# When v is loaded, how a product is cut, and where a split stands: LSH attention and expert layers on one core

## The chip, the cores and the metric

One NeuronCore of a Trainium2 chip runs the whole program. The metric is the device time of one execution in microseconds; before the change it is 791.69 us, the median of 3 runs (791.14 to 792.95).

## The reference

For 2 batches of 8 heads (768 rows, 64 columns) the attention is masked by hashes: q and k are multiplied by a 64 x 6 matrix, the signs are six bits, and a score counts only where the bits of q and of k agree. The result goes through 4 experts (512 to 1024 to 512) whose outputs are added with normalized weights.

```python
mask = q_bucket[:, :, :, None] == k_bucket[:, :, None, :]
scores = np.where(mask, scale * q @ k.T, -1e9)
attn = softmax(scores)
x = (attn @ v), heads side by side           # (1536, 512)
for e in range(4):
    out += p[:, e:e+1] * (np.maximum(x @ w1[e], 0) @ w2[e])
```

## The kernel before

**Attention** (`attention`, from line 470 on) runs over all 16 heads of both batches in steps: six tiles t of 128 rows each make one head, so a step is a (batch, head, t). In each step a list of letters, `ORDER = "VUXSRMENP"`, issues one piece each of several stages, some of them lagging behind by a fixed number of steps:

- S, `stage_s`: TensorE multiplies q by k into a large PSUM tile `sps` (lines 357 and 359, two matmuls of 384 columns each); VectorE takes the minimum with the mask's bound into `p` (line 364).
- E, `stage_e`, one step later: ScalarE's exponential (line 380).
- X, `stage_x`, two steps later in batch 0: VectorE turns blocks of 32 x 32 of `p` into `pt` (line 411).
- N, `stage_n`, three steps behind the end of a head: VectorE's reciprocal of the sums, and SyncE stores it in a row in DRAM (line 392). R, `stage_r`, one step later: SyncE loads that row back, broadcast over 64 partitions, as `rdb` (line 399).
- V, `stage_v`, from three steps behind the end of the odd head of a pair: TensorE multiplies the turned probabilities of both heads by v (line 428), 192 small matmuls (the trace has two records for each) that go to four row groups and two column groups of the array. In batch 0 the product of the first three pairs is cut into `V_PARTS` = 4 parts, one a step; the last pair of batch 0 and batch 1 have it in one.
- U, `stage_u`: ScalarE brings the product from PSUM to `xf` (line 449). M, `stage_m`: POOL multiplies it by `rdb` and splits it in a high and a low part, in two halves (lines 458, 460, 463).
- P: one piece of `prep_head`, which prepares the next head while this one is under way. Transposes of q and k into PSUM (`tps`, line 298), a split in high (ScalarE, line 229) and low (VectorE, line 230) parts, copies on POOL (line 220), the hash matmuls (`hps`, line 314), ScalarE's sign (line 322), POOL's bits (line 328) and a copy. The two large PSUM tiles in flight (pool `ps2`) serve `sps`, `tps` and `hps` in turn. In P also stand two loads on SyncE: q and k of the head after the next at t = 1 (`load_qk`, line 200), and v of the next head at t = 4:

```python
if t == 4 and x + 1 < len(hseq):
    load_v(*hseq[x + 1])
```

`load_v` (line 208) issues four DMAs of 192 KB, one for each group of 32 partitions, into a tile `tv` of which there are two. SyncE takes its instructions in order: one that waits holds up all behind it.

**Expert layers** (`moe`, `second_layer`, and `moe_fast` for batch 1) multiply in high and low parts, three matmuls for one. Weights come through `load_w` (line 553, SyncE) into two buffers `ws` and are split by `split_w`.

**The driver** at the end runs attention of batch 0 alone, with the first weights' split among its steps; then the expert layers of batch 0, into which the steps of batch 1's attention are put by cost: a step counts 652, a product `2 * PV_COST`, and after each group of matmuls so many steps follow as keep the ratio `ATT_PACE * n_att / n_moe`, where `n_att` contains `PV_COST` too. Then come batch 1's expert layers alone.

Of the kernel before, what the change touches and what calls it, by code (L numbers as in the profile page):

```python
# [22 lines left out]
LAG_R = 4  # L23
LAG_X = (2, 3)
LAG_V = (3, 4)
V_PARTS = 4
PV_COST = 3840
PP_BUFS = 4
QK_AT = 1
BLOCKS_FROM = 11  # L30
# [14 lines left out]
def tile_lsh_attention__then__domain_moe(  # L45
# [12 lines left out]
    B, H, S, D = q.shape  # L58
# [37 lines left out]
    def big(name):  # L96
        return ps2.tile([P, 2, 512], F32, tag="big", name=name)

    def one(name):
        return ps1.tile([P, 512], F32, tag="one", name=name)  # L100
# [15 lines left out]
    def two(t):  # L116
        return t.rearrange("p (a n) -> p a n", a=2)
# [65 lines left out]
    def in_blocks(b, h):  # L183
        return b * H + h >= BLOCKS_FROM
# [20 lines left out]
    def load_v(b, h):  # L205
        t = ld.tile([P, QD, NT, D], F32, tag="tv", name="tv", bufs=2)
        for a in range(QD):
            nc.sync.dma_start(
                out=t[a * 32 : (a + 1) * 32], in_=v[b, h].rearrange("(r k c) d -> k r c d", r=QD, c=NT)
            )  # L210
        vvs[b, h] = t
# [3 lines left out]
    def stack_tiles(b, h):  # L215
        heads[b, h] = tuple(stk.tile([P, S], F32R, tag=n, name=n) for n in ("q1", "al", "ah", "k2"))
        return heads[b, h]

    def copy_pool(dst, src):
        nc.gpsimd.tensor_scalar(out=dst, in0=src, scalar1=1.0, scalar2=1.0, op0=ALU.mult, op1=ALU.mult)  # L220
# [7 lines left out]
    def split_half(dst_hi, dst_lo, src):  # L228
        nc.scalar.activation(dst_hi, src, ACTF.Copy, scale=qk_scale)  # L229
        nc.vector.scalar_tensor_tensor(  # L230
            out=dst_lo, in0=src, scalar=qk_scale, in1=dst_hi.bitcast(F32), op0=ALU.mult, op1=ALU.subtract
        )
# [49 lines left out]
    def prep_head(b, h):  # L282
        second = (b, h) == (0, 1)
        if not second:
            tqk = loaded.pop((0, b, h))
        q1, al, ah, k2 = stack_tiles(b, h)
        if second:
            for ps, sl in zip(in_psum, halves):
                split_half(ah[:, sl], al[:, sl], ps[:, :NH])
        elif in_blocks(b, h):  # L290
            xt = ld.tile([P, S], F32, tag="tqk", name="xt")
            nc.vector.transpose(out=xt, in_=tqk.rearrange("p c r d -> p (c r d)"))
            yield 0
            split_half(two(ah), two(al), two(xt))
        else:
            ps = big("tps")
            for c in range(NT):
                nc.tensor.transpose(
                    ps[:, c // 3, (c % 3) * P : (c % 3 + 1) * P], tqk[:, c].rearrange("p a d -> p (a d)"), ident
                )  # L300
            split_half(two(ah), two(al), ps[:, :, :NH])
        for rows in (slice(0, D), slice(D, P)):
            copy_pool(q1[rows], ah[0:D].bitcast(F32))
        copy_pool(k2[0:D], ah[D:P].bitcast(F32))
        yield 654
        if second:
            yield 0
            ps = [one("hps1") for _ in range(2)]
        else:
            hps = big("hps")  # L310
            ps = [hps[:, i] for i in range(2)]
        for j, (w, a) in enumerate(((phi, ah), (plo, ah), (phi, al))):
            for i, sl in enumerate(halves):
                nc.tensor.matmul(ps[i][:MKE, :NH], w, a[:, sl], start=j == 0, stop=j == 2)  # L314
        copy_pool(ah[0:D], al[D:P].bitcast(F32))
        if second:
            for i, sl in enumerate(halves):
                nc.scalar.activation(
                    k2[D:MKE, sl], ps[i][D:MKE, :NH], ACTF.Sign, bias=sgn_bias[D:MKE], scale=SGN_SCALE
                )  # L320
        else:
            nc.scalar.activation(
                two(k2[D:MKE]), hps[D:MKE, :, :NH], ACTF.Sign, bias=sgn_bias[D:MKE], scale=SGN_SCALE
            )
        yield 978
        if b and h and not in_blocks(b, h):
            yield 0
        nc.gpsimd.tensor_scalar(
            out=al[D:MKE],
            in0=k2[D:MKE].bitcast(F32),  # L330
            scalar1=1.0,
            scalar2=bit_mul[D:MKE],
            op0=ALU.add,
            op1=ALU.mult,
        )
        copy_pool(k2[MQ:MQE], al[MK:MKE].bitcast(F32))
        yield 0
# [3 lines left out]
    for j in range(KD):  # L341
        t = xp.tile([P, 2, S], F32R, tag=f"x{j}", name="xs0")
# [70 lines left out]
    def parts_of(b, h):  # L413
        return 1 if b or h >= PB else V_PARTS

# [21 lines left out]
    def stage_u(b, j):  # L437
        banks = pvs.pop((b, j))
        for i in range(2):
            vvs.pop((b, 2 * j + i))  # L440
            pts.pop((b, 2 * j + i))
        if b:
            x = xraw[:, j]
        else:
            xf[j] = xs.tile([P, S], F32, tag="xf", name="xf", bufs=1)
            x = xf[j]
        xv = x.rearrange("p (t a q) -> p a t q", t=NT, q=32)
        for a in range(QD):
            nc.scalar.activation(xv[:, a], banks[a][:, : NT * 32].rearrange("p (t q) -> p t q", q=32), ACTF.Copy)
# [19 lines left out]
    hseq = [(b, h) for b in range(B) for h in range(H)]  # L469
# [3 lines left out]
    def attention():  # L473
        n = len(seq)
        prep = [iter(())]

        def do(op, i):
            if op == "N":
                j = i - LAG_N
                if 0 <= j < n and j % NT == NT - 1:  # L480
                    stage_n(*seq[j][:2])
            elif op == "R":
                j = i - LAG_R
                if 0 <= j < n and j % NT == NT - 1:
                    stage_r(*seq[j][:2])
            elif op == "X":
                for b, lag in enumerate(LAG_X):
                    j = i - lag
                    if 0 <= j < n and seq[j][0] == b:
                        stage_x(*seq[j])  # L490
            elif op == "S":
                if i < n:
                    b, h, t = seq[i]
                    if t == 0:
                        x = hseq.index((b, h))
                        prep[0] = prep_head(*hseq[x + 1]) if x + 1 < len(hseq) else iter(())
                    stage_s(b, h, t)
                    return 652
                return DRAIN
            elif op in "VUM":  # L500
                for back in range(min(LAG_V), max(LAG_V) + V_PARTS + 3):
                    j = i - back
                    if not 0 <= j < n or j % NT != NT - 1 or seq[j][1] % 2 == 0:
                        continue
                    b, h, _ = seq[j]
                    part, parts = back - LAG_V[b], parts_of(b, h)
                    if op == "V" and 0 <= part < parts:
                        stage_v(b, h // 2, part, parts)
                        return 2 * PV_COST * b
                    if op == "U" and part == (0 if b else parts):  # L510
                        stage_u(b, h // 2)
                    for g in range(G if op == "M" else 0):
                        if part == (parts if (b, h) == (0, H - 1) else (1 if b else 1 + parts) + g):
                            stage_m(b, h, g)
            elif op == "E":
                j = i - LAG_E
                if 0 <= j < n:
                    stage_e(*seq[j])
            elif op == "P":
                if i < n:  # L520
                    b, h, t = seq[i]
                    c = next(prep[0], None) if t >= PREP_AT else None
                    x = hseq.index((b, h))
                    if t == QK_AT and x + 2 < len(hseq):
                        load_qk(*hseq[x + 2])
                    if t == 4 and x + 1 < len(hseq):
                        load_v(*hseq[x + 1])
                    return c
            return None

        for i in range(n + max(LAG_V) + 4):
            for op in ORDER:
                c = do(op, i)
                if c is not None:
                    yield c
# [345 lines left out]
    with tc.manual_schedule():  # L881
# [6 lines left out]
        i = 0  # L888
# [13 lines left out]
        for _ in sp:  # L902
            pass
        n_att = H * (NT * 652 + 1632 + PV_COST) + (max(LAG_V) + 4) * DRAIN
        n_moe = NU * (NS * FC * 1960 + NS * TS * 2600)
        for b in range(B):
            dm = da = 0.0
            for c in (moe_fast if b else moe)(b, b * NU):
                dm += c
                while da < dm * ATT_PACE * n_att / n_moe:  # L910
                    x = next(att, None)
# [34 lines left out]
```

## Time and profile before

| | |
|---|---|
| median of 3 runs | 791.69 us (791.14 to 792.95) |
| the profiled execution | 791.18 us, its span 789.4 us |
| TensorE (PE), busy | 725.6 us, 92% |
| VectorE (DVE) | 478.0 us, 61% |
| ScalarE (ACT) | 276.1 us, 35% |
| GpSimd (POOL) | 303.6 us, 38% |
| mean granted clock of TensorE | 0.931 |

The span is the time from the first to the last instruction of the profiled execution; 1.8 us of its own time lie around it. Stages are found by when their lines run: batch 0's attention alone ends near 187 us (first expert matmul with all its inputs), batch 1's attention is over by 500. A matmul's duration in the timeline contains its fill, so the distance between starts is read for what one occupies. "x96" counts the trace's records merged in one line, and the bracket at the end of a line is the idle time ahead of it and what ended it.

### The profile page before, as it was taken

The page shows a single profiled execution, that of the slowest core. Times are in us where ns is not written, and L with a number is a line of the kernel's source. Part 1 is how long each engine was busy: PE and PEld are TensorE (multiplying, and loading weights), DVE is VectorE, ACT ScalarE, POOL GpSimd, SP SyncE. Part 2 cuts the span into 40 slices and gives each one's busy share as a digit, 9 for nine tenths or more (in the row PEclk, how much of TensorE's full clock was granted, in tenths as well). Part 3 has the DMA queues.
Part 4 walks back from the last instruction along what each step waited for, and adds up shares of the span by engine and source line. Part 5 has one row for each costly group of instructions (what it writes and reads, how often), then busy time and mean ns, then how long its engine had stood idle before and what let it go on. Part 6 is the DMA issues. An engine that isn't in the chain of part 4 may idle for free.

```text
span 789.4 us, 14887 instructions
## 1 busy us (share of the span) xinstructions
PE 725.6 (92%) x6232; PEld 645.3 (82%) x6232; DVE 478.0 (61%) x766; ACT 276.1 (35%) x542; POOL 303.6 (38%) x279
## 2 busy tenths in 40 slices
PE   7777858685999999999989999999999999999998
PEld 5556646575989898898979989989899899898896
DVE  7846556523662784378158523387776866866853
ACT  5545444421521342053213202044353343433430
POOL 5326263513331551345134114384342433423520
PEclk9685859586999999999999999999999999999999
DMA  9035151625005420740324212224212212312212
GB/s 209 16 63 106 43 126 38 158 49 84 11 2 115 131 57 2 177 111 13 74 77 103 65 55 64 56 77 136 80 54 81 81 53 57 104 45 64 72 36 81
DMA packets 65554, 59.75 MB, mean 76 GB/s; under 512 B 38224, under 2 KB 46672, under 8 KB 65488
## 3 DMA queue, kind: packets, MB, share of 16 engines
q1 hardware_dynamic: 64464, 58.48, 29.1%
q8 instruction: 49, 0.80, 0.4%
q10 hardware_dynamic: 1024, 0.33, 0.2%
q14 instruction: 17, 0.14, 0.1%
HBM read 55.60 MB, written 3.19 MB: 74 GB/s over the span
## 4 chain that ended last, share of the span: by engine, by line
PE 81%; DVE 5%; POOL 4%; issue 4%; DMA 3%; ACT 2%; SPq 1%; DVEq 0%; POOLq 0%; ACTq 0%
PE mps L603 11%; PE mps L604 11%; PE mps L605 11%; PE pv L428 8%; PE mps L664 5%; PE mps L663 5%; PE mps L665 5%; PE sps L359 3%; PE sps L357 3%; PE hps L314 3%; PE mps L818 2%; PE mps L814 2%; PE mps L817 2%; DMA tqk<-in_k_dram 2%; DVE al L230 1%
## 5 line engine op out<-in xcount | busy, mean ns | idle before, releaser
L603 PE MATMUL mps<-w2hi,hb 128*128 128x512 f32 (+1 forms) x388 | 150.9, 389 | 0.0
L604 PE MATMUL mps<-w2lo,hb 128*128 128x512 f32 (+1 forms) x388 | 150.5, 388 | 0.0
L605 PE MATMUL mps<-w2hi,hb 128*128 128x512 f32 (+1 forms) x388 | 150.5, 388 | 0.0
L380 ACT ACTIVATE p<-p,nb 128x768 f32<-128x768 f32 x96 | 89.6, 933 | 74.4 <-DVE p L364 74.1
L364 DVE TENSOR_SCALAR_CACHE_REDUCE p<-sps 128x768 f32<-128x768 f32 x96 | 89.0, 927 | 38.8 <-PE sps L359 38.8
L597 DVE SCALAR_TENSOR_TENSOR acc<-mps,pe,acc 128x512 f32<-128x512 f32 (+1 forms) x85 | 62.9, 741 | 67.1 <-PE mps L605 66.9
L669 ACT ACTIVATE hb<-mps 128x384 fp32r<-128x384 f32 x64 | 31.4, 491 | 204.8 <-PE mps L665 204.8
L663 PE MATMUL mps<-xs,w1hi 128*128 128x384 f32 x256 | 87.7, 343 | 13.4 <-POOL xs L460 10.6
L411 DVE STREAM_TRANSPOSE pt<-p 128x768 f32<-128x768 f32 x96 | 92.7, 965 | 0.4 <-ACT p L380 0.4
L664 PE MATMUL mps<-xs,w1hi 128*128 128x384 f32 x256 | 87.3, 341 | 0.4 <-POOL xs L463 0.4
L665 PE MATMUL mps<-xs,w1lo 128*128 128x384 f32 x256 | 87.1, 340 | 0.0
L605 PEld LDWEIGHTS mps<-w2hi,hb 128*128 128x128 f32 x388 | 72.8, 188 | 15.9
L603 PEld LDWEIGHTS mps<-w2hi,hb 128*128 128x128 f32 x388 | 72.8, 188 | 14.4 <-issue 0.8
L604 PEld LDWEIGHTS mps<-w2lo,hb 128*128 128x128 f32 x388 | 72.9, 188 | 14.0
L800 POOL TENSOR_TENSOR w2lo<-ws,w2hi 128x512 fp32r<-128x512 f32 x32 | 40.5, 1283 | 105.8 <-ACT w2hi L799 105.8
L564 POOL TENSOR_TENSOR w1lo<-ws,w1hi 128x512 fp32r<-128x512 f32 x32 | 41.8, 1308 | 91.2 <-DVE w1hi L572 74.3
L428 PE MATMUL pv<-pt,tv 32*64 32x192 f32 x3072 | 73.4, 336 | 3.2 <-issue 3.0
L428 PEld LDWEIGHTS pv<-pt,tv 32*64 32x64 f32 x3072 | 64.1, 136 | 11.8 <-issue 10.6
L564 POOL TENSOR_TENSOR w2lo<-ws,w2hi 128x512 fp32r<-128x512 f32 x32 | 41.1, 1287 | 82.8 <-DVE w2hi L572 41.3
L357 PE MATMUL sps<-ah,q 128*128 128x384 f32 x192 | 61.8, 408 | 9.1 <-DVE p L364 7.5
L670 DVE SCALAR_TENSOR_TENSOR hb<-mps,hb 128x384 fp32r<-128x384 f32 x64 | 35.2, 554 | 56.8 <-ACT hb L669 56.6
L220 POOL TENSOR_SCALAR q<-ah 64x768 fp32r<-64x768 f32 (+1 forms) x33 | 27.8, 843 | 104.8 <-ACT ah L229 103.5
(127 smaller groups left out, 1287.5 us busy)
## 6 DMA issues: line engine op xcount, KB each, us to landing
ws<-in_moe_w_dram SPq DMA_DIRECT2D x64, 512.0 KB, 3.7
tv<-in_v_dram SPq DMA_DIRECT2D x64, 192.0 KB, 4.6
rdb<-row SPq DMA_DIRECT2D x16, 192.0 KB, 3.5
out_dram<-acc SPq DMA_DIRECT2D x11, 256.0 KB, 2.1
tqk<-in_q_dram SPq DMA_DIRECT2D x10, 192.0 KB, 5.7
tqk<-in_k_dram SPq DMA_DIRECT2D x10, 192.0 KB, 5.7
tqk<-in_q_dram SPq DMA_DIRECT2D x12, 96.0 KB, 4.2
tqk<-in_k_dram SPq DMA_DIRECT2D x10, 96.0 KB, 4.8
```

The lines of the kernel that those rows point to most:

```text
L357: nc.tensor.matmul(ps[:, i, :NH], q1[:, sl], k1[:, i * NH : (i + 1) * NH], start=True, stop=False)
L364: nc.vector.tensor_scalar(out=two(pt), in0=ps[:, :, :NH], scalar1=MASKED, scalar2=MASKED, op0=ALU.min, op1=ALU.min, accum_out=nb,)
L380: nc.scalar.activation(pt, pt, ACTF.Exp, bias=nb, scale=-1.0, accum_out=den[:, t : t + 1])
L411: nc.vector.transpose(out=pts[b, h][:, :, t], in_=p.rearrange("p (k n) -> p k n", n=32))
L428: nc.tensor.matmul(pvs[b, j][a][i * D : (i + 1) * D, : NT * 32], vvs[b, 2 * j + i][rows, r, c], pts[b, 2 * j + i][rows, k].rearrange("p t ...
L564: nc.gpsimd.tensor_tensor(out=lo[:, c - 1], in0=st[c - 1], in1=hi[:, c - 1].bitcast(F32), op=ALU.subtract)
L603: nc.tensor.matmul(ps, hh[:, ts], w2hi[:, f, cs], start=n == 0, stop=False)
L604: nc.tensor.matmul(ps, hh[:, ts], w2lo[:, f, cs], start=False, stop=False)
L605: nc.tensor.matmul(ps, hl[:, ts], w2hi[:, f, cs], start=False, stop=n == FC - 1)
L663: nc.tensor.matmul(ps[:, :SB], w1hi[:, kk, fs], xhi[b, kk][:, sl], start=kk == 0, stop=False)
L664: nc.tensor.matmul(ps[:, :SB], w1hi[:, kk, fs], xlo[b, kk][:, sl], start=False, stop=False)
L665: nc.tensor.matmul(ps[:, :SB], w1lo[:, kk, fs], xhi[b, kk][:, sl], start=False, stop=kk == KD - 1)
```

## The change

Three edits and a cost. `load_v` of the next pair's two heads is called in `stage_u`, right behind the ScalarE copies that take the product from PSUM; of the calls in P only that for head 1 of batch 0 is left. The product of batch 0's first three pairs is cut in two parts. In `prep_head` for batch 0 the generator gives way once more between the transposes and the split, and once between the hash matmuls and the sign, so that each of the latter is issued one step later. `PV_COST` is 1950 where it was 3840; it is used in batch 1's pacing alone.

```diff
-V_PARTS = 4
-PV_COST = 3840
+V_PARTS = 2
+PV_COST = 1950
@@ prep_head
                 nc.tensor.transpose(
                     ps[:, c // 3, (c % 3) * P : (c % 3 + 1) * P], tqk[:, c].rearrange("p a d -> p (a d)"), ident
                 )
+            if not b:
+                yield 0
             split_half(two(ah), two(al), ps[:, :, :NH])
...
         else:
+            if not b:
+                yield 0
             nc.scalar.activation(
                 two(k2[D:MKE]), hps[D:MKE, :, :NH], ACTF.Sign, bias=sgn_bias[D:MKE], scale=SGN_SCALE
             )
@@ stage_u
         for i in range(2):
             vvs.pop((b, 2 * j + i))
             pts.pop((b, 2 * j + i))
+            nxt = b * H + 2 * j + 2 + i
+            if nxt < len(hseq):
+                load_v(*hseq[nxt])
@@ attention, P
-                    if t == 4 and x + 1 < len(hseq):
-                        load_v(*hseq[x + 1])
+                    if (b, h, t) == (0, 0, 4):
+                        load_v(0, 1)
```

SyncE's queue around the second pair's product (heads 2 and 3), before. The first `tv` is v of head 4, `tqk` q and k of head 6, the second `tv` v of head 5; `row` and `rdb` are the reciprocals of head 3.

```order
L208 DMA tv_842<-in_v_dram 32x4x384 x4
L200 DMA tqk_904<-in_q_dram 128x6x64
L200 DMA tqk_904<-in_k_dram 128x6x64
L392 DMA row_972<-rd_970 128x6
L553 DMA ws_976<-in_moe_w2_dram 128x2x512
L399 DMA rdb_826<-row_972 64x768
L208 DMA tv_1098<-in_v_dram 32x4x384 x4
```

The same stretch now, from the broadcast of head 2 (`row_804`) to q and k of head 7 (`tqk_1214`):

```order
L403 DMA rdb_826<-row_804 64x768
L560 DMA ws_883<-in_moe_w2_dram 128x2x512
L200 DMA tqk_892<-in_q_dram 128x6x64
L200 DMA tqk_892<-in_k_dram 128x6x64
L396 DMA row_1008<-rd_1006 128x6
L403 DMA rdb_826<-row_1008 64x768
L208 DMA tv_1129<-in_v_dram 32x4x384 x4
L208 DMA tv_1134<-in_v_dram 32x4x384 x4
L200 DMA tqk_1214<-in_q_dram 128x6x64
L200 DMA tqk_1214<-in_k_dram 128x6x64
```

Both v loads (heads 4 and 5) stand together behind the broadcast of head 3, and q and k of head 6 (`tqk_892`) no longer stand behind a v load but behind a load of weights; those of head 7 now stand behind both v loads.

TensorE in the even head of the second pair, before, from the transposes for the next head on:

```order
L298 MATMUL tps<-ident,tqk 128x128 x6
L357 MATMUL sps<-ah,q_753 128x384 x2
L359 MATMUL sps<-k_756,al 128x384 x2
L314 MATMUL hps<-ah,phi 108x384 x2
L314 MATMUL hps<-ah,plo 108x384 x2
L314 MATMUL hps<-al,phi 108x384 x2
L428 MATMUL pv<-pt,tv 64x192 x48
L357 MATMUL sps<-ah,q_753 128x384 x2
L359 MATMUL sps<-k_756,al 128x384 x2
L428 MATMUL pv<-pt,tv 64x192 x48
L357 MATMUL sps<-ah,q_753 128x384 x2
L359 MATMUL sps<-k_756,al 128x384 x2
```

And now:

```order
L298 MATMUL tps<-ident,tqk 128x128 x6
L361 MATMUL sps<-ah,q_759 128x384 x2
L363 MATMUL sps<-k_762,al 128x384 x2
L432 MATMUL pv<-pt,tv 64x192 x96
L361 MATMUL sps<-ah,q_759 128x384 x2
L363 MATMUL sps<-k_762,al 128x384 x2
L316 MATMUL hps<-ah,phi 108x384 x2
L316 MATMUL hps<-ah,plo 108x384 x2
L316 MATMUL hps<-al,phi 108x384 x2
L432 MATMUL pv<-pt,tv 64x192 x96
L361 MATMUL sps<-ah,q_759 128x384 x2
L363 MATMUL sps<-k_762,al 128x384 x2
```

The hash matmuls stand one score further back, and 96 instead of 48 small matmuls stand between two scores.

SyncE at the last pair of batch 0, before (the reciprocals and the broadcast of head 7 ahead of the v load of head 9):

```order
L392 DMA row<-rd 128x6
L399 DMA rdb<-row 64x768
L208 DMA tv<-in_v_dram 32x4x384 x4
L191 DMA tqk<-in_q_dram 32x24x32 x2
```

And now, where the v loads of heads 8 and 9 have come between the two:

```order
L396 DMA row<-rd 128x6
L208 DMA tv<-in_v_dram 32x4x384 x8
L403 DMA rdb<-row 64x768
L191 DMA tqk<-in_q_dram 32x24x32 x2
```

## Rows read from the trace of the kernel before

**Rows 1.** Windows by stage: us, then busy us (count) of each engine, clock, DMA share, GB/s

```profile
20.00:187.00 167.00, 119.96 (x1822) 96.32 (x1822) 90.81 (x156) 70.89 (x140) 67.48 (x76) 0.70 0.36 79
...
187.00:500.00 313.00, 305.05 (x2902) 279.04 (x2902) 176.43 (x302) 87.65 (x182) 113.91 (x101) 0.99 0.28 70
```

**Rows 2.** SyncE's queue: waits from 20 to 200 us: total, times, longest

```profile
SPq L208 <- PE pv L428: 82.4, 4, 22.3
```

**Rows 3.** Waits of TensorE from 20 to 200 us: total, times, longest

```profile
PE tps L298 <- DMA tqk<-in_k_dram: 18.7, 3, 6.3
...
PE sps L359 <- POOL k L220: 5.9, 3, 2.7
```

**Rows 4.** Timeline near the second pair's end: start us, duration, engine, line, tiles, idle before

```profile
94.08 1.75 SPq L208 DMA_DIRECT2D tv<-in_v_dram  x4
...
95.73 0.08 DVE L364 DVE_READ_ACCUMULATOR p<-sps 128x1 f32 x1
...
96.47 0.65 SPq L200 DMA_DIRECT2D tqk<-in_k_dram  x1
...
101.75 1.51 PE L298 MATMUL tps<-ident,tqk 128*128 128x128 f32 x6 [6.24 <-DMA tqk<-in_k_dram]
```

**Rows 5.** Timeline: transposes of five heads, starts (preparing heads 2, 3, 7, 8, 9)

```profile
19.87 1.54 PE L298 MATMUL tps<-ident,tqk 128*128 128x128 f32 x6 [0.23 <-DVE p L364]
...
32.97 1.54 PE L298 MATMUL tps<-ident,tqk 128*128 128x128 f32 x6 [0.68 <-DVE p L364]
...
117.80 1.48 PE L298 MATMUL tps<-ident,tqk 128*128 128x128 f32 x6
...
141.90 1.51 PE L298 MATMUL tps<-ident,tqk 128*128 128x128 f32 x6 [6.29 <-DMA tqk<-in_k_dram]
...
156.67 1.48 PE L298 MATMUL tps<-ident,tqk 128*128 128x128 f32 x6
```

**Rows 6.** Timeline, VectorE: two minima a step apart; the low part of a split

```profile
112.55 0.92 DVE L364 TENSOR_SCALAR_CACHE_REDUCE p<-sps 128x768 f32<-128x768 f32 x1
...
114.30 0.92 DVE L364 TENSOR_SCALAR_CACHE_REDUCE p<-sps 128x768 f32<-128x768 f32 x1
...
120.38 1.02 DVE L230 SCALAR_TENSOR_TENSOR al<-tps,qk_scale,ah 128x768 fp32r<-128x768 f32 x1 [1.38 <-ACT ah L229]
```

**Rows 7.** Timeline: the first part of a product; one step of a later product

```profile
39.29 3.67 PE L428 MATMUL pv<-pt,tv 32*64 32x192 f32 x96
...
127.84 0.62 PE L357 MATMUL sps<-ah,q 128*128 128x384 f32 x2
...
128.75 2.21 PE L428 MATMUL pv<-pt,tv 32*64 32x192 f32 x96
...
130.88 0.62 PE L357 MATMUL sps<-ah,q 128*128 128x384 f32 x2
...
131.89 0.96 DVE L364 TENSOR_SCALAR_CACHE_REDUCE p<-sps 128x768 f32<-128x768 f32 x1 [1.18 <-PE sps L359]
```

**Rows 8.** Windows: a head with a product and a late transpose; one without

```profile
117.80:143.06 25.26, 18.22 (x427) 15.10 (x426) 12.96 (x22) 9.15 (x19) 8.00 (x9) 0.84 0.32 70
...
143.06:156.67 13.61, 11.31 (x33) 8.67 (x31) 10.81 (x18) 8.00 (x15) 10.45 (x12) 0.50 0.65 155
```

**Rows 9.** Timeline behind the last product of batch 0

```profile
172.57 1.75 SPq L208 DMA_DIRECT2D tv<-in_v_dram  x4
...
175.65 1.50 SPq L392 DMA_DIRECT2D row<-rd  x1
...
181.15 0.48 SPq L399 DMA_DIRECT2D rdb<-row  x1
...
184.52 1.18 POOL L458 TENSOR_TENSOR xf<-xf,rdb 128x384 f32<-128x384 f32 x1 [21.61 <-DMA rdb<-row]
```

**Rows 10.** Timeline in the expert layers of batch 0

```profile
396.20 0.43 DVE L572 CAST w2hi<-ws 128x512 fp32r<-128x512 f32 x1 [18.18 <-DMA ws<-in_moe_w_dram]
...
397.21 0.61 PE L663 MATMUL mps<-xs,w1hi 128*128 128x384 f32 x1 [2.76 <-DVE hb L670]
```

## The prediction

> **What bounds the kernel now.** I read the windows by stage first, then the waits, then the timeline at the places that the waits name. The windows [rows 1] split the span. From 187 to 500 us, the expert layers of batch 0 with the attention of batch 1 among them, TensorE (PE) is busy for 305.05 of 313 us at a granted clock of 0.99: little but less PE work helps there, and what follows, the expert layers of batch 1 alone, the change doesn't touch. From 20 to 187 us, the attention of batch 0, it is busy for 119.96 of 167 us at a granted clock of 0.70, and no other engine is full (VectorE, DVE, 90.81 us). That stretch is where the change can pay.
>
> Who holds it up stands in the waits. SyncE's queue spent 82.4 us in 4 waits of the v load (L208) for the product of the pair [rows 2], and PE waited 18.7 us, in 3 waits of some 6.2, for a landing k half of tqk, and 5.9 us, in 3, for GpSimd (POOL) at the score matmuls [rows 3]. The timeline of one pair joins the two [rows 4]: the v load of the next pair, which sits on SyncE's queue behind nothing but a buffer that this pair's product reads, gets through at 94.08; only then can the q and k of a later head be issued, k at 96.47; it lands 5.2 us later, and the transposes that need it start at 101.75. The PSUM buffer that these transposes take was read out at 95.73 + 0.08 = 95.81, so 5.94 us of the gap is the queue's.
>
> Transposes to transposes, heads 2 to 7 took 156.67 - 32.97 = 123.7 us, 41.2 a pair, and a head with neither product nor late transposes 32.97 - 19.87 = 13.1 us [rows 5]. VectorE's own pace is a step of 114.30 - 112.55 = 1.75 us and 1.02 us a head for the low part of the split [rows 6]: 12 x 1.75 + 2 x 1.02 + 0.4 for two reciprocals = 23.4 us a pair, well below 41.2. So no engine sets the pace; the chain of waits does.
>
> **The change part by part.**
>
> *The v load behind the evacuation.* The order shows it: ahead of the q and k that an even head's step 1 issues no v load stands any more, at most a load of weights, whose buffer POOL frees some four steps before. The 8 v loads now stand behind the pair's last product on TensorE, which is next in the program anyway, so SyncE is held there only as long as TensorE itself is. The q and k of [rows 4] would go out some 5 steps before they are needed. Three waits of 5.94 us go: **-17.8 us**. Late next is VectorE with its 1.75 a step, which is what the next terms are made against. Behind the v loads stand, in an odd head, q and k, the reciprocals' row and its broadcast; none is due before step 5 of that head.
>
> *POOL's waits.* In before, the multiplications of a finished pair (two groups of three operations) come in steps 1 and 2 of the odd head, wait for the broadcast of the reciprocals, which SyncE held back too, and push the sign's two operations behind the next head's scores. With the product done in two steps they come in step 5 of the even head and step 0 of the odd one, after one head's sign operations and before the next's. The 5.9 us of [rows 3] go: **-5.9 us**.
>
> *Split and sign a step later* (six prepared heads, 2 to 7). VectorE stood 1.38 us for ScalarE's high part, which itself had waited for the transposes of the same step [rows 6]. A step later those are long done, but the split then holds one of the two large PSUM buffers until VectorE has read it, so TensorE can run one step less ahead. Between 0 and 1.4 us a head; I take 0.8, since the high part still stands behind an exponential on ScalarE: **-4.8 us**. The two POOL operations behind the sign end a step later, about 1 us before the next head's scores want them; I cost that at nothing, and its cover is the one spare step.
>
> *Product in two parts.* The instructions are the same; what moves is how well VectorE is fed. In before, a product step is TensorE's: scores from 127.84 to 128.75, a part from 128.75 to 130.88, then the next scores, 3.04 us, and VectorE stands 1.18 us in it [rows 7]. Four are 12.2 us. Now two steps have 0.91 + 2 x 2.13 = 5.17 us, and the two that are freed run at VectorE's 1.75: 2 x 5.17 + 2 x 1.75 = 13.8. **+1.7 us a pair, +5.0 us** for three. Below, nothing (TensorE runs ahead in the slack); above, a part that begins at the low clock: 96 records took 3.67 us there against 2.21 [rows 7], 1.46 more on the second half of the first part, 4.4 us for three pairs.
>
> *Start of the expert layers.* The last pair's reciprocals travel to memory and back: v loads at 172.57, row at 175.65, broadcast at 181.15, POOL released at 184.52, 11.95 us behind the end of the product [rows 9]. In the new order the row goes out first, but 8 v loads (twice the 1.75 us of issuing, and 1,536 KB) stand between it and the broadcast. [rows 4] give the rate: 6 transfers of 192 KB, 1,152 KB, from 94.08 to 101.75, 150 KB a us. 1,536 KB take 10.2 us, and with 2 ahead (VectorE's minimum, the reciprocals, the row's issue) and 1.3 for the broadcast's own 192 KB it lands some 13.7 us behind the product, 1.8 later than now; if the transfers share the engines rather than queue, issue at 6.1 + 3.4 gives 9.5, 2.5 earlier. I take **+1 us**, nearer to the queue that [rows 4] show.
>
> *Batch 1.* The same SyncE wait made VectorE, and with it TensorE, late by 2.76 us at 397.21 [rows 10]: VectorE had stood 18.18 us for weights whose load was queued behind v. That goes: **-2.8 us** (bounds 0 and -3.5). The smaller PV_COST spreads attention steps and expert matmuls in another ratio; the work is the same and TensorE is full there, so I cost it at nothing. What covers it is TensorE's own queue of ready work; if it fails, waits like this one come in its place.
>
> **Sum.** -17.8 - 5.9 - 4.8 + 5.0 + 1 - 2.8 = -25.3 us. The profiled execution took 791.18 us (span 789.4, 1.8 around it), 0.5 below the median 791.69 of the runs, within their spread. 791.18 - 25.3 = 765.9: **766 us**. A pair would then take (123.7 - 17.8 - 5.9 - 4.0 + 5.0) / 3 = 33.7 us, or 13.1 and 20.6 for its two heads.
>
> **The rivals.**
>
> *The low clock stays: slower.* [...] **4%**.
>
> *The q and k are late again, behind v.* 8 v loads and a q and k are 1,920 KB, 12.8 us at the rate of rows 4, 16.2 with a load of weights (512 KB) among them. From the end of the product to the next even head's transposes there are about nine steps of 1.75 and a split, 17 us. For it: no row shows ten such transfers in a row, and in the new order q and k of the odd head stand behind all 8. Against: 1 to 4 us of slack. Some 3 us a pair: **775 us**, 13%.
>
> *The two parts eat more.* Both halves of the first part at the low clock, nothing from the later split, half of POOL's waits back: 4.4 + 4.8 + 3: **778 us**, 10%.
>
> *It doesn't take the wait away.* The q and k are late for another reason: only the 2.8 and a little more are gained, **788 us**, 2%. The order speaks against it.
>
> **How the numbers follow.** The forecast has 71%. Its low end: product parts at no cost (-5.0), 1.4 instead of 0.8 a head (-3.6), broadcast early (-3.5), 754 if all come together; the high end is the third rival with batch 1 gaining nothing, 781. The range 756 to 779 takes in the forecast's likely part and most of the second and third rival. A measurement here can tell 0.2%, 1.6 us, from no change. Faster 0.93, same 0.02, slower 0.05.
>
> **What would show it.** Right: no wait of transposes for tqk in 20 to 187 us; SyncE's waits of the v load short, and before q and k none; expert layers' first matmul some 23 us earlier; POOL no releaser of scores; product steps near 5.2 us on TensorE with VectorE idle 2 to 4 us in each. Wrong: the stage still ends at 187 us, or the granted clock in it falls below 0.70, or new waits in 187 to 500 us exceed 5 us.

## The result and the profile after

The changed kernel took **772.78 us** (median of 4 runs, 768.57 to 774.39) against 792.01 us of the kernel before (4 runs beside it, 791.14 to 792.95): a ratio of 0.9749, 95% interval 0.9708 to 0.9789. It is faster by 2.5%, where 766.0 us (756 to 779) had been forecast. The profiled execution took 772.6 us, its span 770.9 us, 18.5 us less than the 789.4 us before.

The page of the changed kernel, busy time of each engine and the granted clock in 40 slices of the span:

```profile
PE 720.2 (93%) x6232; PEld 643.3 (83%) x6232; DVE 473.2 (61%) x766; ACT 276.8 (36%) x542; POOL 303.9 (39%) x279
...
PEclk9587887759999999999999999999999999999999
```

The windows, cut where [rows 5] and [rows 8] cut them before, at the transposes that a head starts with: head 1, heads 2 to 7, and then the stretch from 187 us on, as in [rows 1].

```profile
20.42:34.28 13.86, 11.31 (x37) 9.22 (x37) 11.73 (x21) 8.27 (x15) 5.04 (x6) 0.61 0.33 63
34.28:137.03 102.75, 86.57 (x1369) 70.32 (x1369) 71.16 (x124) 56.32 (x110) 56.68 (x63) 0.78 0.50 102
...
187.00:500.00 313.00, 303.27 (x2913) 277.31 (x2912) 167.96 (x296) 83.80 (x175) 113.56 (x98) 1.00 0.28 73
```

The same view of the kernel before, heads 2 to 7:

```profile
32.97:156.67 123.70, 91.58 (x1369) 73.35 (x1369) 72.65 (x124) 57.02 (x113) 56.81 (x63) 0.69 0.39 86
```

Heads 2 to 7 take 102.75 us where they took 123.7, at a clock of 0.78 instead of 0.69. So a pair takes 34.25 us, not 41.2. That is more than the whole gain. The account of the 18.5 us of span, stretch by stretch:

| stretch | before us | after us | difference |
|---|---|---|---|
| up to head 2's transposes | 32.97 | 34.28 | +1.3 |
| heads 2 to 7 | 123.70 | 102.75 | -20.95 |
| from head 8's transposes to the second matmul of the expert layers (L664 at 187.44, now L671 at 168.42) | 30.77 | 31.39 | +0.6 |
| the rest | 601.96 | 602.48 | +0.5 |

TensorE's waits from 15 to 200 us, which answer to [rows 3] (total, times, longest):

```profile
PE sps L361 <- DVE p L368: 16.2, 26, 1.1
PE mps L670 <- POOL xs L467: 12.3, 1, 12.3
PE tps L298 <- DVE p L368: 4.3, 6, 0.7
```

No transposes wait for a landing any more, and no score matmuls for POOL. What is left is VectorE's minimum, that is, the pace of the pipeline, and the start of the expert layers. SyncE's queue, from 20 to 200 us, in place of the 82.4 us of [rows 2]:

```profile
SPq L396 <- DVE rd L394: 118.2, 9, 30.7
...
SPq L208 <- PE pv L432: 5.2, 3, 2.2
```

The queue still waits, now 118.2 us for the reciprocals (22.0 us before), but no transfer that TensorE needs is late by it: none of TensorE's waits names a DMA. The last reading is of TensorE's waits from 200 to 520 us, the expert layers of batch 0 with the attention of batch 1 in them. Here is something that was not forecast. A wait for "issue" is a pause for which the profile shows nothing that the engine waited for; the first row is of the kernel before, the others are of the changed kernel:

```profile
PE pv L428 <- issue: 3.0, 4, 1.1
```

```profile
PE pv L432 <- issue: 8.1, 7, 1.7
...
PE mps L670 <- issue: 0.6, 1, 0.6
```

The wait for late weights of [rows 10] is gone, but the pauses without any releaser inside the products have grown from 3.0 us in 4 to 8.1 us in 7.

### The profile page after: what moved, and what is told of

Its sections match the earlier page's. It is cut to its first block, busy times and chain, and to the rows that moved or that the text cites. A ratio compares the mean times of both kernels' runs of the same rounds, so it can differ in the third digit from the quotient of the medians.

```text
span 770.9 us, 14888 instructions
## 1 busy us (share of the span) xinstructions
PE 720.2 (93%) x6232; PEld 643.3 (83%) x6232; DVE 473.2 (61%) x766; ACT 276.8 (36%) x542; POOL 303.9 (39%) x279
## 4 chain that ended last, share of the span: by engine, by line
PE 87%; DVE 8%; issue 2%; DMA 2%; ACT 0%; POOL 0%; ACTq 0%; SPq 0%; POOLq 0%; DVEq 0%
PE mps L610 11%; PE mps L612 11%; PE mps L611 11%; PE pv L432 10%; PE mps L671 6%; PE mps L670 6%; PE mps L672 6%; PE sps L361 4%; DVE p L368 4%; PE sps L363 4%; DVE pt L415 3%; PE hps L316 3%; PE mps L825 2%; PE mps L821 2%; PE mps L824 2%
## 5 line engine op out<-in xcount | busy, mean ns | idle before, releaser
L670 PE MATMUL mps<-xs,w1hi 128*128 128x384 f32 x256 | 87.2, 341 | 12.9 <-POOL xs L467 12.3
L671 PE MATMUL mps<-xs,w1hi 128*128 128x384 f32 x256 | 87.0, 340 | 0.4 <-POOL xs L470 0.4
L610 PEld LDWEIGHTS mps<-w2hi,hb 128*128 128x128 f32 x388 | 72.9, 188 | 13.8 <-issue 0.6
L432 PEld LDWEIGHTS pv<-pt,tv 32*64 32x64 f32 x3072 | 66.0, 140 | 16.5 <-issue 14.8
L361 PE MATMUL sps<-ah,q 128*128 128x384 f32 x192 | 60.7, 401 | 17.8 <-DVE p L368 16.6
L361 PEld LDWEIGHTS sps<-ah,q 128*128 128x128 f32 x192 | 37.1, 216 | 33.5 <-DVE p L368 18.1
```

What stands on the lines that cost most here:

```text
L361: nc.tensor.matmul(ps[:, i, :NH], q1[:, sl], k1[:, i * NH : (i + 1) * NH], start=True, stop=False)
L432: nc.tensor.matmul(pvs[b, j][a][i * D : (i + 1) * D, : NT * 32], vvs[b, 2 * j + i][rows, r, c], pts[b, 2 * j + i][rows, k].rearrange("p t ...
L610: nc.tensor.matmul(ps, hh[:, ts], w2hi[:, f, cs], start=n == 0, stop=False)
L670: nc.tensor.matmul(ps[:, :SB], w1hi[:, kk, fs], xhi[b, kk][:, sl], start=kk == 0, stop=False)
L671: nc.tensor.matmul(ps[:, :SB], w1hi[:, kk, fs], xlo[b, kk][:, sl], start=False, stop=False)
```

## The experiments

Two questions were asked of the first four runs. In heads 2 to 7: is it the place of the v load that pays, or the more regular order of the other edits? In the rest: do the pauses in the products come with the smaller PV_COST? The next three went after what the first left open, and the last put together what had helped. Diffs are against the changed kernel, but for the first, which starts from the kernel before. All ratios are to the kernel before, run beside them on the same chip (793.07 us in the first four, 792.13 us in the others, 11 runs each). The changed kernel's 772.78 us was measured apart from them and its interval is some 3 us to either side, so a small difference to it is read in the traces, stretch by stretch, as well.

**Before, with the v load moved and nothing else**

```diff
 stage_u
             pts.pop((b, 2 * j + i))
+            nxt = b * H + 2 * j + 2 + i
+            if nxt < len(hseq):
+                load_v(*hseq[nxt])
 attention, P
-                    if t == 4 and x + 1 < len(hseq):
-                        load_v(*hseq[x + 1])
+                    if (b, h, t) == (0, 0, 4):
+                        load_v(0, 1)
```

> The kernel before with the v loads moved alone (product in four parts, no later split or sign, PV_COST 3840). Theory A, the load's place is what pays: the three late transposes go (-17.8 us), so 771 to 775 us. Rival B, it needs the other edits (POOL's multiplications still come in the odd head and push the sign's operations): half of it, 778 to 783 us, with waits of scores for POOL near 5.9 us again.

Measured: 774.24 us (771.23 to 774.95), ratio 0.976 [0.9733, 0.9786], as good as the whole change. The windows of this kernel, head 1 and heads 2 to 7, and the row of TensorE's score matmuls that wait for POOL, from 15 to 200 us:

```profile
21.07:34.56 13.49, 11.36 (x36) 8.77 (x36) 11.67 (x21) 8.15 (x15) 5.05 (x6) 0.63 0.16 37
34.56:137.54 102.98, 77.75 (x1369) 60.80 (x1370) 72.66 (x124) 56.86 (x113) 56.89 (x63) 0.88 0.48 105
```

```profile
PE sps L359 <- POOL k L220: 9.4, 3, 3.6
```

Heads 2 to 7 fall by 123.70 - 102.98 = 20.7 us and no transposes wait for a landing. POOL's waits did not go with the v load; they rose from 5.9 [rows 3] to 9.4 us. The clock of the stretch rose to 0.88, and TensorE's own busy time fell from 91.58 us in before to 77.75 for the same 1369 matmuls. So 13.8 us of the 20.7 are shorter busy time and only 32.12 - 25.23 = 6.9 us less idle time (the stretch less the busy time in each): as the 18.7 us of waits for landings went, those of scores for VectorE's minimum rose from 2.5 to 9.7 us in this stretch, beside POOL's. The change gave more than the length of the waits that went. How much of that is the clock's own worth no run separates: with four parts and the step between, further down, the stretch takes 5.0 us less at a lower clock, 0.83.

**Without the step between**

```diff
                 )
-            if not b:
-                yield 0
             split_half(two(ah), two(al), ps[:, :, :NH])
...
         else:
-            if not b:
-                yield 0
             nc.scalar.activation(
```

> The changed kernel with split and sign back at their old steps. Prediction's term: the lag is worth 4.8 us, so 777 us. Rival: the lag only trades VectorE's wait for the high part against TensorE's wait for the PSUM buffer that the split holds (1.06 us waits of scores for VectorE in the changed kernel's timeline), so 771 to 774 us, and head 1 takes 13.1 us again instead of 13.9.

Measured: 778.17 us (777.11 to 779.0), ratio 0.9817 [0.9792, 0.9843]. The windows, head 1 and heads 2 to 7:

```profile
20.36:33.61 13.25, 9.93 (x36) 7.47 (x36) 11.80 (x21) 8.04 (x15) 5.04 (x6) 0.76 0.13 33
33.61:140.05 106.44, 90.88 (x1368) 71.33 (x1369) 70.83 (x124) 55.85 (x110) 56.63 (x63) 0.76 0.47 97
```

The step between is worth 106.44 - 102.75 = 3.7 us over heads 2 to 7, and costs 13.86 - 13.25 = 0.6 us in head 1. By the medians it is worth 5.4 us, near the 4.8 of the prediction; in this trace the last product of batch 0 also took longer (10.17 us, 8.94 in the changed kernel), and so did the pauses in the products of batch 1 (9.4 us, 8.1). In head 1, and in other heads without a product (again at 60.43 us), the timeline of the changed kernel shows the price: scores that wait for the PSUM buffer that the split still holds.

```profile
24.87 1.01 PE L361 MATMUL sps<-ah,q 128*128 128x384 f32 x2 [1.06 <-DVE p L368]
```

**The product in four parts again**

```diff
-V_PARTS = 2
+V_PARTS = 4
```

> The changed kernel with the product of batch 0 in four parts. Prediction's term: two parts cost 5.0 us for three pairs, so 768 us. Rival: with four parts the multiplications come two steps later, in the odd head, and what the finer parts give is lost in POOL's queue, 772 to 776 us.

Measured: 768.8 us (767.56 to 770.37), ratio 0.9701 [0.9675, 0.9728]: four parts are better than two. The window of heads 2 to 7, and POOL among TensorE's waits from 15 to 200 us:

```profile
34.14:132.13 97.99, 82.94 (x1369) 66.07 (x1369) 72.86 (x124) 57.53 (x113) 56.95 (x63) 0.83 0.50 108
```

```profile
PE sps L363 <- POOL k L220: 4.4, 3, 1.9
```

The three runs and the changed kernel make a table of four, us for heads 2 to 7, all with the v load moved:

| | four parts | two parts |
|---|---|---|
| no step between | 102.98 | 106.44 |
| step between | 97.99 | 102.75 |

The step between pays 5.0 or 3.7 us. Two parts cost 3.5 or 4.8 us, although POOL's waits of 9.4 or 4.4 us go with them: the product's steps themselves cost that much more. Each cell is one trace; four later runs that leave this stretch as in the changed kernel have 101.3 to 104.0 us there, and the last run, with four parts and the step, has 97.99 again. Neither edit is needed to remove the wait; the v load's place alone did that. Where the two parts lose can be seen in the second pair of the changed kernel, TensorE and VectorE on its timeline, then the window of the first part's beginning (the clock is the third number from the end):

```profile
71.58 0.62 PE L361 MATMUL sps<-ah,q 128*128 128x384 f32 x2 [0.87 <-DVE p L368]
...
72.56 5.68 PE L432 MATMUL pv<-pt,tv 32*64 32x192 f32 x192
...
78.17 0.62 PE L361 MATMUL sps<-ah,q 128*128 128x384 f32 x2
...
79.18 0.96 DVE L368 TENSOR_SCALAR_CACHE_REDUCE p<-sps 128x768 f32<-128x768 f32 x1 [3.65 <-PE sps L363]
...
80.12 4.16 PE L432 MATMUL pv<-pt,tv 32*64 32x192 f32 x192
...
85.22 0.96 DVE L368 TENSOR_SCALAR_CACHE_REDUCE p<-sps 128x768 f32<-128x768 f32 x1 [4.12 <-PE sps L363]
```

```profile
72.56:75.00 2.44, 2.44 (x65) 2.10 (x72) 2.33 (x4) 2.26 (x5) 1.34 (x2) 0.50 0.04 8
```

The first part takes 5.68 us, the second, of as many matmuls, 4.16: the first begins at a granted clock of 0.50 (72.56 to 75.00 us), after scores between which TensorE stood, and the second runs at 1.00 (80.12 to 84.21 us). VectorE stands 3.65 and 4.12 us, where a step of four parts cost it 1.18 [rows 7]. From the scores at 71.58 to those behind the second part (84.21) it is 12.6 us for two steps, where 10.3 had been worked out. Of these 2.3 us, 1.35 are the first part (78.17 - 72.56 = 5.61 where 4.26 was reckoned), and 1.1 are the hash matmuls, which the later split has put between the two parts (78.98 to 80.12 us) and which the sum left out.

**PV_COST as before**

```diff
-PV_COST = 1950
+PV_COST = 3840
```

> The changed kernel with PV_COST 3840, so that only the pacing of batch 1's attention is as before. Prediction's term: nothing, 772 to 774 us. Rival, that the pacing decides which weight loads run beside the products and so how long TensorE stands without instructions in them (8.1 us in the changed kernel, 3.0 before): 3 to 5 us less, 768 to 770 us, with those waits back near 3 us.

Measured: 769.74 us (767.41 to 771.73, 6 runs), ratio 0.9705 [0.9679, 0.9732]; its first row of TensorE's waits from 200 to 520 us:

```profile
PE pv L432 <- issue: 4.6, 4, 1.7
```

The median is 3.0 us below that of the changed kernel, as the rival had it, though the ranges of the two overlap; the pauses, 4.6 us where there were 8.1, go the same way. The traces of five kernels say it more firmly. From the second matmul of the expert layers to the end, the changed kernel and the two runs above with the cost at 1950 take 602.5, 602.7 and 602.5 us, with pauses of 8.1, 9.4 and 8.3 us in the products; this run and the first one, with 3840, take 598.5 and 599.7 us, with pauses of 4.6 and 4.8 us. A number that only sets the pace of equal work is thus not free: it costs some 3 to 4 us here. Why, the timeline of batch 1's first product in the changed kernel shows, TensorE first, then SyncE's queue:

```profile
217.69 2.86 PE L432 MATMUL pv<-pt,tv 32*64 32x192 f32 x128
221.61 2.86 PE L432 MATMUL pv<-pt,tv 32*64 32x192 f32 x128 [1.06 <-issue]
226.16 2.86 PE L432 MATMUL pv<-pt,tv 32*64 32x192 f32 x128 [1.69 <-issue]
229.62 0.45 PE L670 MATMUL mps<-xs,w1hi 128*128 128x384 f32 x1 [0.59 <-issue]
...
214.89 22.41 SPq L560 DMA_DIRECT2D ws<-in_moe_w_dram  x3
237.39 4.32 SPq L208 DMA_DIRECT2D tv<-in_v_dram  x8
```

The pauses stand exactly 128 of the trace's matmuls apart (with their 128 weight loads, 256 instructions; 64 matmuls of the program), and loads of weights run beside the first two runs of 128. The transfers from 215 to 232 us, the strip of the DMA engines' busy share in 40 slices and the queue that the page calls `instruction`:

```profile
DMA  0000806998000002589630000000010000001000
...
q8 instruction: 4, 0.07, 1.4%
```

The queue moved 0.07 MB in 4 packets, 16,384 bytes each by the trace's list of packets, about one for each run of 128. I take it for TensorE's queue, an inference from counts: the whole execution has 49 of these blocks, and 49 x 256 = 12,544 is close to TensorE's 6232 matmuls and 6232 weight loads, while no other engine on the page has as many as 1000 instructions. A slice is 0.425 us, so the strip stands at 6 to 9 from 217.6 to 219.3 and at 5 to 9 from 221.8 to 223.5, each time while the run ahead of a pause goes on. By the list of packets the three blocks within the product begin to come at 219.17, 223.72 and 227.33 us: the first two as a burst of loads ends, 1.48 and 2.11 us behind the start of the run ahead, the third with no load left, 1.17 us behind it. They have landed at 220.17, 224.71 and 228.28 us, and TensorE goes on 1.44, 1.45 and 1.34 us after that. The third pause, 0.59 us, has no load beside it, so not all of the pauses is the loads' doing. The same product, of 385 or 386 matmuls, in the windows of the changed kernel and of the kernel before, where no load ran beside it (DMA share 0.26 and 0.03) and where it still paused once:

```profile
217.70:229.60 11.90, 8.57 (x385) 7.53 (x384) 0.89 (x2) 0.49 (x1) 2.12 (x2) 1.00 0.26 90
```

```profile
229.60:239.70 10.10, 8.88 (x386) 7.93 (x385) 0.75 (x1) 0.00 (x0) 0.21 (x1) 1.00 0.03 5
...
237.49 2.20 PE L428 MATMUL pv<-pt,tv 32*64 32x192 f32 x93 [1.15 <-issue]
```

From this came a theory for the next runs: the small matmuls of the product use up instructions faster than the rest, and where big loads fill the DMA engines the next block of instructions comes late. Its rival: the pauses belong to the product as it is written, whatever runs beside it.

**v of batch 1 one step earlier, ahead of the weights**

```diff
             nxt = b * H + 2 * j + 2 + i
-            if nxt < len(hseq):
+            if nxt < len(hseq) and not b:
                 load_v(*hseq[nxt])
...
-                    stage_n(*seq[j][:2])
+                    b, h, _ = seq[j]
+                    stage_n(b, h)
+                    if b and h % 2 and h + 1 < H:
+                        load_v(b, h + 1)
+                        load_v(b, h + 2)
```

> The changed kernel with the v loads of batch 1 put on SyncE's queue one step earlier, ahead of the weight loads that now run beside the products of batch 1; nothing else differs. Theory C: TensorE uses up its instructions in a product and their refill is late when a weight load runs beside it; held weights let it come in time. Waits without a releaser inside products fall from 8.1 us to 3 to 4 us and the time to 768 to 770 us, unless held weights are missed later (a wait of TensorE for a split, 1 to 3 us). Rival D: the gaps belong to the product's own instructions and where it stands; 8 us and 772 to 774 us stay.

Measured: 768.42 us (767.84 to 770.08), ratio 0.9707 [0.9684, 0.973]. The v load, which must wait for the product, now holds the weights' loads back until it is over. Timeline of the same product, SyncE's queue, and the pauses from 200 to 520 us:

```profile
216.87 5.46 PE L432 MATMUL pv<-pt,tv 32*64 32x192 f32 x256
222.50 2.86 PE L432 MATMUL pv<-pt,tv 32*64 32x192 f32 x128 [0.18 <-issue]
225.96 0.44 PE L674 MATMUL mps<-xs,w1hi 128*128 128x384 f32 x1 [0.59 <-issue]
...
225.47 4.90 SPq L208 DMA_DIRECT2D tv<-in_v_dram  x8
230.47 10.35 SPq L564 DMA_DIRECT2D ws<-in_moe_w_dram  x3
```

```profile
PE pv L432 <- issue: 2.8, 5, 0.9
```

Two pauses are left here, of 0.18 us and, behind the product, of 0.59 us, again 128 matmuls apart; over 200 to 520 us the products have 2.8 us of them instead of 8.1. The wait of [rows 10] is back, but at 1.3 us instead of 2.8. TensorE's instructions and their order are the same; only what moves beside them changed. So 5.3 us of the pauses come from the loads, as the theory has it. The other 2.8 us stay, in this product with no load beside them, and so the rival holds in part as well.

**Batch 1's product in four pieces among the expert matmuls**

```diff
                     if op == "V" and 0 <= part < parts:
+                        if b:
+                            return [(h // 2, k) for k in range(PV_PIECES)]
                         stage_v(b, h // 2, part, parts)
-                        return 2 * PV_COST * b
+                        return 0
...
-                if c is not None:
+                if isinstance(c, list):
+                    for j, k in c:
+                        stage_v(1, j, k, PV_PIECES)
+                        yield 2 * PV_COST / PV_PIECES
+                elif c is not None:
```

> The changed kernel with each product of batch 1 in four pieces with expert matmuls between (same instructions, same loads). Theory C: the pieces of 96 records no longer outrun the refill, waits without a releaser near 0 to 2 us, 766 to 768 us. Rival D: if they belong to the product's instructions themselves, 772 to 774 us; VectorE and ScalarE, whose scores have to wait for the PSUM that the product holds longer, could take some of it back.

Measured: 765.28 us (765.04 to 765.52), ratio 0.9665 [0.9641, 0.9689]. The window around the first such product, the same window of the changed kernel, and the only wait of TensorE that is left from 200 to 520 us:

```profile
213.00:233.00 20.00, 20.00 (x364) 18.42 (x363) 4.85 (x13) 3.54 (x7) 7.08 (x7) 1.00 0.26 81
```

```profile
213.00:233.00 20.00, 16.65 (x431) 15.36 (x430) 3.70 (x9) 2.37 (x4) 3.37 (x3) 1.00 0.18 56
```

```profile
PE sps L362 <- ACT xraw L457: 1.0, 1, 1.0
```

TensorE is busy for all of the 20 us, beside three loads of weights and a higher DMA share (0.26 instead of 0.18). No pause is left when 96 of the small matmuls, fewer than 128, follow each other: the other side of the theory, the rate at which instructions are used, bears it out too. The lists of packets suggest why pauses stay even without loads. In the traces of the kernel before and of the changed kernel, 49 blocks each, no two of this queue begin to come less than 3.28 us apart (3.28 in the first, 3.36 in the second), while a further 128 of the small matmuls took 5.46 - 2.86 = 2.60 us in the run above. So, by this estimate, the product by itself uses up its blocks faster than they came in either trace; and with loads beside it TensorE stood 1.06 and 1.69 us at the first two steps from one run of 128 to the next, against none and 0.18 with the loads held back.

**The broadcast ahead of batch 1's first v loads**

```diff
-            if nxt < len(hseq):
+            if nxt < len(hseq) and (b, j) != (0, H // 2 - 1):
                 load_v(*hseq[nxt])
...
                     stage_r(*seq[j][:2])
+                    if seq[j][:2] == (0, H - 1):
+                        load_v(1, 0)
+                        load_v(1, 1)
```

> The changed kernel with the 8 v loads behind the last product of batch 0 put behind the broadcast of its reciprocals. If the broadcast's transfer stands in line behind v (issued at 158.61, POOL released at 165.50), it lands 4 to 6 us earlier, the wait of the first expert matmul for POOL falls from 12.3 to 7 or 8 us and the time to 767 to 769 us. If the transfers share the engines, 771 to 773 us.

Measured: 766.3 us (762.49 to 770.96, 6 runs, a wide spread, and the profiled execution is the fastest), ratio 0.968 [0.9649, 0.971]. First the start of the expert layers in the changed kernel, then in this one:

```profile
142.93 8.94 PE L432 MATMUL pv<-pt,tv 32*64 32x192 f32 x384
...
154.35 4.04 SPq L208 DMA_DIRECT2D tv<-in_v_dram  x8
158.61 0.48 SPq L403 DMA_DIRECT2D rdb<-row  x1
...
165.50 1.18 POOL L465 TENSOR_TENSOR xf<-xf,rdb 128x384 f32<-128x384 f32 x1 [22.17 <-DMA rdb<-row]
```

```profile
140.75 10.38 PE L432 MATMUL pv<-pt,tv 32*64 32x192 f32 x384
...
155.41 0.48 SPq L403 DMA_DIRECT2D rdb<-row  x1
155.98 3.86 SPq L208 DMA_DIRECT2D tv<-in_v_dram  x8
...
158.81 1.18 POOL L465 TENSOR_TENSOR xf<-xf,rdb 128x384 f32<-128x384 f32 x1 [17.66 <-DMA rdb<-row]
```

From the issue of the broadcast to POOL's release it is 165.50 - 158.61 = 6.9 us behind the eight v loads and 158.81 - 155.41 = 3.4 us ahead of them. In the changed kernel the landing itself comes 6.7 us after the issue. The fastest of its other broadcasts in batch 0 lands after 3.2 us, so the 3.4 us leave some 0.2 us at most that the loads issued right behind can have cost. So here the broadcast stood in line behind transfers that were issued first; it did not share with them on equal terms. TensorE's wait for POOL falls from 12.3 to 6.3 us.

**All that helped: four parts, the pieces, the broadcast first**

> The changed kernel with the product of batch 0 in four parts (768.8 us by itself), that of batch 1 in four pieces, and the broadcast ahead of v. If the gains add, 4.0 + 5 to 6 + 4 to 5: 757 to 760 us. If two of them buy the same time, 763 to 766 us.

Measured: **754.18 us** (753.88 to 755.22), ratio 0.9526 [0.9502, 0.955], 18.6 us below the changed kernel. The three edits alone gave 4.0, 7.5 and 6.5 us by the medians, 18.0 together (by the ratios 3.8, 6.7 and 5.5 us, 16.0 together, against 17.7 for all three in one kernel). The time came out some 3 us below the range, since the pieces and the broadcast each gave more than was put in. In the traces heads 2 to 7 take 97.99 us instead of 102.75, the start of the expert layers 25.48 instead of 31.39 and the rest 595.06 instead of 602.48: the edits lie in different stretches and add up. Of TensorE's waits from 15 to 200 us these are left, beside 11.4 us for VectorE's minimum:

```profile
PE mps L680 <- POOL xs L468: 6.3, 1, 6.3
PE sps L364 <- POOL k L221: 3.7, 3, 1.5
```

What was not tried: the changed kernel with the v load at its old place.

## Why the prediction was right, and where its sizes were off

The mechanism held, by its own signs: no transposes wait for tqk, SyncE's waits of the v load are 5.2 us in all, POOL releases no scores, the second matmul of the expert layers starts 187.44 - 168.42 = 19.0 us earlier (some 23 were expected of the first). One sign that would have spoken against it came true as well, new waits of more than 5 us from 187 to 500 us. The sum was 25.3 us; the span gave 18.5. Step by step:

- **The v load behind the evacuation, -17.8:** the load alone gave -20.7 us in heads 2 to 7. The waits that ended last were rightly counted. What was left out is, on one side, that TensorE's busy time fell by 13.8 us at a clock of 0.88 instead of 0.69, and on the other that waits for VectorE (7.2 us more) and POOL (3.5 us more) came in their place; what the clock alone is worth was not measured. The loads stand in `stage_u` ahead of ScalarE's copies, not behind them; what they wait for on SyncE is the product's matmuls, the 5.2 us above.
- **POOL's waits, -5.9, and the product in two parts, +5.0:** the two belong to one edit, and -0.9 was expected of them together. Measured, four parts against two with all else equal, +4.8 us. POOL's waits did go; the two parts cost, gross, an estimate of 4.8 + 4.4 = 9.2 us in place of 5.0. This is the mis-sized term of the attention stage: the upper bound, a part that begins at the low clock, was in the text and was not taken, and the first parts took 5.7 to 6.1 us where 4.26 (twice 2.13) was reckoned. The hash matmuls between the parts, 1.1 us in the second pair, were in no term. A part of this is the third rival.
- **Split and sign a step later, -4.8:** -3.7 in heads 2 to 7 by the run without it (-5.0 with four parts), where the term held -4.0. For the sixth, prepared in head 1, where -0.8 was reckoned, it costs 0.6. The reason against, named with the term, that TensorE can run one step less ahead, is what the 1.06 us at 24.87 shows. The same stretch also began later by some 0.5 us, but that start varies from 19.7 to 21.1 us among the runs.
- **The start of the expert layers, +1:** +0.6. POOL was released 165.50 - 151.87 = 13.6 us behind the product; the queue estimate was 13.7 (its terms, 2 + 10.2 + 1.3, add up to 13.5), and the run with the broadcast first shows that the queue is the right picture. The rest was given back by the product before it, 8.94 us instead of 10.00. That is in part luck: the same product took from 9.0 to 10.7 us in the later runs where it had no pause. The clock rose from 0.50 to 1.00 1.1 us into it in the changed kernel (at 144.00 us) and 2.7 us into it in before (at 165.21).
- **Batch 1, -2.8:** +0.5, the largest miss of one term, 3.3 us. The run with the v load alone splits it: the stretch takes 599.7 us there, 2.3 less than before, near the -2.8 of the wait of [rows 10], and 602.5 us in the changed kernel, 2.8 more. "I cost it at nothing" failed: with another pacing, the products of batch 1 came to run beside loads of weights. TensorE's queue of ready work, named as the cover, was no cover: TensorE stood in the products for pauses with no releaser (8.1 us), and went on 1.34 to 1.45 us after a block had landed.

Together the misses are 1.8 in heads 2 to 7, 2.1 ahead of them, -0.4 at the start of the expert layers and 3.3 behind it, 6.8 us, which is 25.3 less 18.5. In heads 2 to 7 the small miss is a balance of larger ones, -2.9 us for the load, +5.7 for POOL's waits with the two parts and -1.0 for the step between (by the run with four parts); that the sum came near there is partly luck. Of the rivals, the one by which the clock stays low is out: the clock of heads 2 to 7 rose from 0.69 to 0.78, and with the v load alone to 0.88. In part the low clock stayed, since head 1 still runs at 0.61 and the second pair's first part begins at 0.50; but with the long waits taken away the clock of the stretch rose. What lowers it, no run separates. The rival by which q and k are late behind v is out too: none of TensorE's waits names them.

On the pauses in the products, the runs together: with the product in pieces none was left; with the loads held back 2.8 us of pauses stayed, up to 0.9 us each; with loads of weights beside the product, two of them took 1.06 and 1.69 us. That they are waits for the next block of instructions is my reading of blocks of 16,384 bytes and of pauses 256 instructions apart.

## What to carry to other kernels

Look for a transfer that waits for a buffer and holds up its queue, as the v load did SyncE's (82.4 us, [rows 2]), and ask what stands behind it: moving it to where its buffer is already free gave 2.4% here by itself, more than the waits it ended. Edits that come along with such a move want a run each, since one of these (two parts) cost 4 us and a pacing constant took some 3 more. A long run of very small matmuls was better cut up and mixed with larger ones here (7.5 us by the medians, with loads of weights beside it), and a small transfer that an engine waits for was better put ahead of the big ones that nobody waits for yet (6.5 us).

## What the runs showed of the hardware that was not expected

- TensorE paused with nothing that the profile shows to wait for; my reading is that it had run out of instructions. In the first product of batch 1 it stood every 128 matmuls with their 128 weight loads, for 1.06 and 1.69 us when 512 KB loads ran beside it, and for 0.59 us when they had ended; for 0.18 and 0.59 us with the loads held back; not at all with the product cut into four pieces. In the changed kernel it went on 1.34 to 1.45 us after a block of 16,384 bytes had landed, and in the traces of the two kernels, before and changed, blocks began to come at least 3.28 us apart.
- A broadcast issued behind eight transfers of 192 KB released its reader 6.9 us after its issue, ahead of them after 3.4 us: on this queue a transfer waited for those before it, and not for those behind it.
- With three waits of some 6 us gone, the granted clock of a stretch of 100 us rose from 0.69 to 0.88, and the same 1369 matmuls took 77.75 us of TensorE's time instead of 91.58.
